# Linear attention with a mixture of adapters on one core: another spread of a batch's 576 tokens over the partitions, and other places for its loads

## The chip, the cores and the metric

The kernel runs on one core of a Trainium2 chip. The metric is the device time of one execution in microseconds (us), as the median of several executions. The engines are PE (TensorE), DVE (VectorE), ACT (ScalarE), POOL (GpSimd) and SP (SyncE, which here only issues transfers).

## What is computed

Two stages in a row, cut from the reference. The first is linear attention with position weights over 8 batches, 8 heads, 576 tokens and a head size of 64; the second is a gated mixture of 8 adapters of rank 16, of which the two with the highest logits count.

```python
def phi(x, c, s):                       # c, s: cos and sin of the position
    r = np.maximum(x, 0.0)
    return np.concatenate([r * c, r * s], axis=-1)
q_p, k_p = phi(q, cos_w, sin_w), phi(k, cos_w, sin_w)
kv = np.einsum('bhsf,bhsd->bhfd', k_p, v)
z = np.sum(k_p, axis=2)
num = np.einsum('bhsf,bhfd->bhsd', q_p, kv)
den = np.einsum('bhsf,bhf->bhs', q_p, z)[..., None] + 1e-06
attn = num / den                        # -> x, (4608, 512)
...
logits = x @ w_gate                     # 8 experts, the top two kept
w = softmax of the two kept logits
out = x + sum over the two: w * ((x @ A[e]) @ B[e])
```

The inputs q, k and v have 9.44 MB each in float32, and the output has 9.44 MB as well.

## The kernel before

**Tiling.** Two batches form a pair, and there are four pairs. A pair has 9 slots; a slot is one token on each of the 128 partitions. `NS` = 9 slots times four pairs make 36 slots, and the main loop goes through them with the index n. The 576 tokens of a batch are spread over 64 partitions: `LONG` = 5 consecutive tokens on each partition of one half, and `SHORT` = 4 on each partition of the other half. The batch with the even number has the lower half in slots 0 to 4 and the upper half in slots 0 to 3; the odd one has the upper half in slots 4 to 8 and the lower half in slots 5 to 8. So slot 4 is shared by both batches, and a slot's work needs one batch, or in slot 4 two.

**Loads.** `load` (L73) issues two transfers for each of k, q and v of a batch (L75): one to 64 partitions with 8 heads of 5 x 64 elements, and one to the other 64 with 8 heads of 4 x 64. One packet is one run of a head in one partition, so k and q move in packets of 1280 and 1024 bytes. k and q go over SP's queue (q1 in the profile) as float32. v goes over POOL's queue (q0) and is cast to bf16 on the way, so its packets read as many bytes as those of k and write half (640 and 512 bytes, which is what the profile counts for q0). The adapter weights A, w_gate and B go over ACT's queue (q10); A moves in packets of 64 bytes.

**Buffers and issue.** The pools for k and q have two buffers, each for a pair, and there are two v buffers, so the loads of pair m wait until pair m-2 is used up. The table `load_at` says at the end of which iteration n the loads of a batch are issued: batches 2 to 7 after n = 0, 2, 6, 10, 15 and 19. SP works its list in order: a load that stands behind a store isn't issued before the store, and a store waits for ACT's copy `osb` (L315). Besides, the transfers of SP and ACT carry eight completion semaphores in turn (DMAHW0 to DMAHW7), and the issuing engine waits before each transfer until the one eight places before it has landed.

**One iteration.** POOL scales q of slot n+3 by the cos and sin tables (`scale_q`, L190); ACT does the same with relu for k (`scale_k`, L149 and L154) of slot n+8, so ACT runs eight slots ahead and is the first to need a new batch; PE adds slot n+6 to the sums (`kv`, L172), transposes q (L198), multiplies (`numden`, L218); DVE moves the transposes out of PSUM (L203, L239) and divides (`normalise`, L225 and L227). Three slots form a group for the gate (`logits`, `gate_a`, `gate_sig`, `gate_b`). Some six slots after `normalise` a slot gets its adapters (`delta`, L306), ACT copies it out (`evac_o`, L315) and SP stores it (`store`, L327) in two transfers of 64 partitions, in packets of 2048 bytes.

**The head.** Before the loop stand the first loads, the position tables (`sin_tab`, `cos_tab`, L104 and L105, on ACT), the weights, and slots 0 to 4 of k, of which slot 4 needs both batches. DVE copies the weights to bf16 there (`AW` L347, `Ball` L348).

Of the kernel before, what the change touches and what calls it, by code (L numbers as in the profile page):

```python
# [19 lines left out]
LONG, SHORT = 5, 4  # L20
# [4 lines left out]
def kernel(ctx, tc, q, k, v, w_gate, A, Bw, out):  # L25
# [11 lines left out]
    LS = LONG * HALF  # L37
    assert S == LS + SHORT * HALF

# [13 lines left out]

    pos = persist.tile([128, NS], mybir.dt.int32, name="pos")
    lo, hi = slice(0, HALF), slice(HALF, 128)
    nc.gpsimd.iota(pos[lo, 0:5], pattern=[[1, 5]], base=0, channel_multiplier=LONG)
    nc.gpsimd.iota(pos[hi, 0:4], pattern=[[1, 4]], base=LS, channel_multiplier=SHORT)
    nc.gpsimd.iota(pos[lo, 5:9], pattern=[[1, 4]], base=LS, channel_multiplier=SHORT)
    nc.gpsimd.iota(pos[hi, 4:9], pattern=[[1, 5]], base=0, channel_multiplier=LONG)
# [4 lines left out]
    def halves(b):  # L64

        if b % 2 == 0:
            return ((lo, 0, LONG, 0), (hi, 0, SHORT, LS))
        return ((hi, 4, LONG, 0), (lo, 5, SHORT, LS))

    def part(dram, b, n, t0):  # L70
        return dram[b, :, t0:t0 + n * HALF, :].rearrange("h (p s) d -> p h s d", s=n)

    def load(eng, dram, t, b):  # L73
        for pr, s0, n, t0 in halves(b):
            eng.dma_start(out=t[pr, :, s0:s0 + n, :], in_=part(dram, b, n, t0))  # L75
# [4 lines left out]
    def load_k(b):  # L80
        m = b // 2
        if b % 2 == 0:
            k_t[m] = p_k.tile([128, H, NS, D], FP32, name="ks")
        load(nc.sync, k, k_t[m], b)

    def load_q(b):
        m = b // 2
        if b % 2 == 0:
            q_t[m] = p_q.tile([128, H, NS, D], FP32, name="qs")
        load(nc.sync, q, q_t[m], b)  # L90

    def load_v(b):
        load(nc.gpsimd, v, v_view(b // 2), b)

    load_k(0)
    load_v(0)
    load_q(0)
# [25 lines left out]

    AWf = persist.tile([128, DCH, ZW], FP32, name="AWf")
    for ci in range(DCH):
        nc.scalar.dma_start(out=AWf[:, ci, 0:ER],
                            in_=A[:, ci * 128:(ci + 1) * 128, :].transpose([1, 0, 2]))
    nc.scalar.dma_start(out=AWf[:, :, ER:ZW], in_=w_gate.rearrange("(c p) e -> p c e", p=128))
    Bf = persist.tile([128, DM], FP32, name="Bf")
    nc.scalar.dma_start(out=Bf, in_=Bw.rearrange("e r d -> (e r) d"))  # L130
    AW = persist.tile([128, DCH, ZW], BF16, name="AW")
    Ball = persist.tile([128, DM], BF16, name="Ball")

    load_k(1)
    load_v(1)
    load_q(1)


# [180 lines left out]
    def store(n):  # L319
        m, s = divmod(n, NS)  # L320
        t = osb_t.pop(n)
        for b in (2 * m, 2 * m + 1):
            for pr, s0, cnt, t0 in halves(b):
                if s0 <= s < s0 + cnt:
                    rows = out[b * S + t0:b * S + t0 + cnt * HALF, :].rearrange(
                        "(p s) d -> p s d", s=cnt)[:, s - s0, :]
                    nc.sync.dma_start(out=rows, in_=t[pr, :])  # L327

# [7 lines left out]
    load_at = {0: 2, 2: 3, 6: 4, 10: 5, 15: 6, 19: 7}  # L336

    with tc.manual_schedule():
        scale_q(0)
        scale_q(1)  # L340
        for j in range(5):
            scale_k(j, both=True)
            kv(j)
        transp_q(0)
        evac_q(0)
        kv_out(0)
        nc.vector.tensor_copy(AW, AWf)  # L347
        nc.vector.tensor_copy(Ball, Bf)  # L348
        scale_q(2)
        transp_q(1)  # L350
        numden(0)

        todo = []
        for n in range(NT + 8):
            live = n < NT
            ready = [g for g, t in enumerate(groups) if t[-1] + 1 == n]
            gated = [g for g, t in enumerate(groups) if t[-1] + 2 == n]
            moved = [g for g, t in enumerate(groups) if t[-1] + 3 == n]
            for g in ready:
                logits(g)  # L360
            for g in gated:
                gate_sig(g)
            if n + 3 < NT:
                scale_q(n + 3)
            if live:
                normalise(n)
            for j in scale_at.get(n, ()):
                if j < NT:
                    scale_k(j)
            for d in todo[:1] if live else todo:  # L370
                delta(d)
                evac_o(d)
                store(d)
            del todo[:1 if live else None]
            if live:
                transp_x(n)
            if n + 1 < NT:
                evac_q(n + 1)
                numden(n + 1)
            if live:  # L380
                evac_x(n)
            if n + 2 < NT:
                transp_q(n + 2)
            for g in moved:
                evac_z(g)
                todo += groups[g]
            for g in ready:
                gate_a(g)
            for g in gated:
                gate_b(g)  # L390
                transp_z(g)
            for j in kv_at.get(n, ()):
                if j < NT:
                    kv(j)
                    if j % NS in (4, 8):
                        kv_out(2 * (j // NS) + (j % NS == 8))
# [36 lines left out]
```

## Time and profile before

| | us |
|---|---|
| median of 3 executions | 165.33 (163.04 to 167.11) |
| the profiled execution, its own time | 166.19 |
| its span, first to last instruction | 164.4 |
| PE, DVE, ACT, POOL busy | 104.3, 89.5, 73.0, 61.4 |

The profiled execution is 1.8 us longer than its span and 0.9 us longer than the median. The share of the DMA engines in the profile is the sum of the times of all packets over 16 engines; packets of several queues, and packets that follow each other in one queue, can overlap, so it goes beyond 100%. The granted TensorE clock was 0.886 in the mean.

### The profile page before, as it was taken

The numbers are of one execution on the slowest core, as the hardware profiler recorded it, in microseconds if no ns is written. First come the engines' busy times: TensorE is split into PE (matmuls) and PEld (weight loads), VectorE is DVE, ScalarE is ACT, GpSimd is POOL, SyncE is SP. The second block draws the span as 40 slices with busy tenths as digits, with TensorE's granted clock in tenths as the row PEclk, the third lists the DMA queues.
The fourth block names the chain that finished last, engine by engine and source line by source line (L and its number), as shares of the span: only waits on it lengthen the run. The fifth ranks groups of instructions, "written<-read, shape, count | busy, mean of one in ns | idle before, by whom it ended". The sixth has DMA issues, their size and how long they took to land. (4 is left out here: it accounts for less than half of the span.)

```text
span 164.4 us, 3588 instructions
## 1 busy us (share of the span) xinstructions
PE 104.3 (63%) x1379; PEld 83.4 (51%) x1396; DVE 89.5 (54%) x273; ACT 73.0 (44%) x130; POOL 61.4 (37%) x98
## 2 busy tenths in 40 slices
PE   0000835994496698598398760198989897956450
PEld 0000834793496476486387640086868685733100
DVE  1001226852388376589368490058897889985200
ACT  3005439038803863683475500557578323213330
POOL 7100458770367057347433660033645363000000
PEclk9999999999559789999959996569999999996755
DMA  5999999999999999999999999999998664452654
GB/s 106 202 257 249 254 242 225 215 249 240 203 237 214 207 255 224 215 262 267 224 224 250 177 233 226 222 314 209 226 241 255 157 157 109 97 128 68 159 121 106
DMA packets 35953, 33.81 MB, mean 206 GB/s; under 512 B 6624, under 2 KB 31200, under 8 KB 35936
## 3 DMA queue, kind: packets, MB, share of 16 engines
q1 hardware_dynamic: 22656, 28.32, 75.3%
q0 software_dynamic: 8448, 4.72, 21.1%
q10 hardware_dynamic: 4832, 0.54, 2.9%
q8 instruction: 11, 0.18, 0.5%
q14 instruction: 6, 0.05, 0.1%
HBM read 28.85 MB, written 9.44 MB: 233 GB/s over the span
## 5 line engine op out<-in xcount | busy, mean ns | idle before, releaser
L190 POOL TENSOR_SCALAR qp<-qs,cos_tab 128x512 bf16<-128x512 f32 x36 | 25.0, 695 | 76.2 <-PE qpTp L198 52.3
L149 ACT ACTIVATE kp<-ks,cos_tab 128x512 bf16<-128x512 f32 x36 | 25.6, 718 | 38.9 <-DMA ks<-in_k_dram 33.4
L172 PE MATMUL kvz<-v,kp 128*128 128x128 bf16 (+1 forms) x320 | 28.4, 246 | 21.6 <-ACT kp L149 16.7
L172 PEld LDWEIGHTS <-kp 128*128 128x128 bf16 (+1 forms) x320 | 23.1, 111 | 23.4 <-ACT kp L149 19.7
L239 DVE COPY xT<-xz 128x512 bf16<-128x512 bf16 x36 | 15.2, 422 | 35.4 <-PE xz L234 34.9
L315 ACT COPY osb<-dx 128x512 f32<-128x512 f32 x36 | 20.7, 576 | 21.1 <-DMA out_dram<-osb 6.7
L306 PE MATMUL dx<-xt,ident 128*128 128x512 bf16 x35 | 14.9, 425 | 19.0 <-ACT osb L315 19.0
L198 PE MATMUL qpTp<-ident,qp 128*128 128x128 bf16 x288 | 25.4, 239 | 0.8 <-DVE qpT L203 0.8
L203 DVE TENSOR_SCALAR qpT<-qpTp 128x1024 bf16<-128x1024 bf16 x36 | 24.5, 682 | 2.2 <-PE qpTp L198 2.2
L227 DVE TENSOR_TENSOR xt<-nd,rden 128x512 bf16<-128x512 f32 x36 | 24.9, 692 | 1.2
L190 POOL TENSOR_SCALAR qp<-qs,sin_tab 128x512 bf16<-128x512 f32 x36 | 25.4, 706 | 0.0
L154 ACT ACTIVATE kp<-ks,sin_tab 128x512 bf16<-128x512 f32 x31 | 22.0, 708 | 0.0
L218 PE MATMUL nd<-kvsb,qpT 128*128 128x65 bf16 (+1 forms) x320 | 18.5, 204 | 4.1 <-ACT kvsb L184 2.3
L198 PEld LDWEIGHTS <-qp 128*128 128x128 bf16 x288 | 19.5, 108 | 1.3 <-issue 1.1
L234 PE MATMUL xz<-ident,xt 128*128 128x128 bf16 x144 | 16.1, 242 | 6.1 <-DVE xt L227 5.0
L234 PEld LDWEIGHTS <-xt 128*128 128x128 bf16 x144 | 11.6, 109 | 15.3 <-DVE xt L227 9.6
L218 PEld LDWEIGHTS <-qpT 128*128 128x128 bf16 (+1 forms) x320 | 14.1, 105 | 6.2 <-DVE qpT L203 3.0
L307 PEld LDWEIGHTS <-zgT 128*128 128x128 bf16 x36 | 3.7, 103 | 21.5 <-issue 21.4
L151 DVE TENSOR_SCALAR kp<-ks,sin_tab 128x512 bf16<-128x512 f32 x5 | 2.6, 565 | 18.6 <-ACT sin_tab L104 14.0
L214 PE MATMUL nd<-eps_hi,ones 128*128 128x4 bf16 x72 | 12.6, 177 | 0.0
L251 PE MATMUL za<-AW,xT 128*128 128x136 bf16 x144 | 11.0, 226 | 0.5 <-DVE xT L239 0.5
L75 POOL DMA_DIRECT2D v<-in_v_dram x16 | 11.2, 704 | 0.0
(41 smaller groups left out, 83.2 us busy)
## 6 DMA issues: line engine op xcount, KB each, us to landing
out_dram<-osb SPq DMA_DIRECT2D x72, 128.0 KB, 3.4
ks<-in_k_dram SPq DMA_DIRECT2D x8, 640.0 KB, 8.3
qs<-in_q_dram SPq DMA_DIRECT2D x8, 640.0 KB, 12.2
ks<-in_k_dram SPq DMA_DIRECT2D x8, 512.0 KB, 9.7
qs<-in_q_dram SPq DMA_DIRECT2D x8, 512.0 KB, 14.3
v<-in_v_dram POOLq DMA_DIRECT2D x8, 320.0 KB, 12.0
v<-in_v_dram POOLq DMA_DIRECT2D x8, 256.0 KB, 14.1
AWf<-in_moe_A_dram ACTq DMA_DIRECT2D x4, 64.0 KB, 9.6
```

Of the source, the lines that this page charges most:

```text
L149: nc.scalar.activation(kp[:, :, 0, :], src, AF.Relu, bias=0.0, scale=cos_tab[:, s:s + 1])
L154: nc.scalar.activation(kp[:, :, 1, :], src, AF.Relu, bias=0.0, scale=sin_tab[:, s:s + 1])
L172: nc.tensor.matmul(out=kvz_t[b][:, gg, jj], lhsT=kp_t[j][pr, h], rhs=v_rhs(m, h, s, pr), start=(first and jj == 0), stop=(last and jj == 3))
L190: nc.gpsimd.tensor_scalar(out=qp[:, :, i, :], in0=q_t[m][:, :, s, :], scalar1=tab[:, s:s + 1], scalar2=1.0, op0=ALU.mult, op1=ALU.mult)
L198: nc.tensor.transpose(out=t[:, h, :], in_=qp[:, h], identity=ident)
L203: nc.vector.tensor_scalar(out=t, in0=src, scalar1=0.0, scalar2=None, op0=ALU.max)
L218: nc.tensor.matmul(out=nd[pr, gg, j * W:(j + 1) * W], lhsT=qpT[:, gg * 4 + j, pr], rhs=kv_t[b][:, gg * 4 + j, :], start=False, stop=(j == ...
L227: nc.vector.tensor_tensor(out=xt, in0=nd[:, :, :, 0:D], in1=rden.rearrange("p (g j) -> p g j", g=2).to_broadcast([128, 2, 4, D]), op=ALU.mult)
L234: nc.tensor.transpose(out=xz[:, c * 128:(c + 1) * 128], in_=xt_t[n][:, c * 128:(c + 1) * 128], identity=ident)
L239: nc.vector.tensor_copy(t, xz[:, 0:512].rearrange("p (c s) -> p c s", c=DCH))
L306: nc.tensor.matmul(out=dx, lhsT=ident, rhs=xt_t.pop(n), start=True, stop=False)
L315: nc.scalar.copy(t, src)
```

## The change

A batch's first 512 tokens (`TAIL` = 512) go four to a partition over all 128 partitions: slots 0 to 3 for the even batch of a pair, slots 5 to 8 for the odd one. Its last 64 tokens go one to a partition into slot 4, the even batch's to the lower half, the odd one's to the upper half. A load becomes `load_main` (128 partitions, 8 heads of 4 x 64 elements, packets of 1024 bytes) and `load_tail` (64 partitions, 8 heads of 64 elements, packets of 256 bytes; for v 512 and 128 bytes as written). A slot's store is one transfer of 128 partitions, but for slot 4. The weights go over SP's queue behind the first k, v and q. `load_at` has the loads of batches 3 to 7 one or three iterations sooner. The copies of the weights to bf16 stand at the end of iteration 1. All instructions, those of the head too, now stand in the order in which they are written.

```diff
-LONG, SHORT = 5, 4
+FOUR = 4
...
-    def load(eng, dram, t, b):
-        for pr, s0, n, t0 in halves(b):
-            eng.dma_start(out=t[pr, :, s0:s0 + n, :], in_=part(dram, b, n, t0))
+    def load_main(eng, dram, t, b):
+        s0 = 0 if b % 2 == 0 else 5
+        eng.dma_start(out=t[:, :, s0:s0 + FOUR, :],
+                      in_=dram[b, :, 0:TAIL, :].rearrange("h (p s) d -> p h s d", s=FOUR))
+
+    def load_tail(eng, dram, t, b):
+        eng.dma_start(out=t[lo if b % 2 == 0 else hi, :, 4, :],
+                      in_=dram[b, :, TAIL:S, :].rearrange("h p d -> p h d"))
...
-    load_k(0)
-    load_v(0)
-    load_q(0)
+    load_main(nc.sync, k, k_t[0], 0)
+    load_main(nc.gpsimd, v, v_view(0), 0)
+    load_tail(nc.sync, k, k_t[0], 0)
+    load_tail(nc.sync, k, k_t[0], 1)
+    load_tail(nc.gpsimd, v, v_view(0), 0)
+    load_main(nc.sync, q, q_t[0], 0)
...
+    load_main(nc.sync, k, k_t[0], 1)
+    load_tail(nc.gpsimd, v, v_view(0), 1)
+    load_main(nc.gpsimd, v, v_view(0), 1)
+    load_tail(nc.sync, q, q_t[0], 0)
+    load_tail(nc.sync, q, q_t[0], 1)
     AWf = persist.tile([128, DCH, ZW], FP32, name="AWf")
     for ci in range(DCH):
-        nc.scalar.dma_start(out=AWf[:, ci, 0:ER],
+        nc.sync.dma_start(out=AWf[:, ci, 0:ER],
...
+    load_main(nc.sync, q, q_t[0], 1)
...
+        if s == 4:
+            for b, pr in ((2 * m, lo), (2 * m + 1, hi)):
+                nc.sync.dma_start(out=out[b * S + TAIL:(b + 1) * S, :], in_=t[pr, :])
+        else:
+            b, i = (2 * m, s) if s < 4 else (2 * m + 1, s - 5)
+            rows = out[b * S:b * S + TAIL, :].rearrange("(p s) d -> p s d", s=FOUR)[:, i, :]
+            nc.sync.dma_start(out=rows, in_=t)
...
-    load_at = {0: 2, 2: 3, 6: 4, 10: 5, 15: 6, 19: 7}
+    load_at = {0: 2, 1: 3, 3: 4, 7: 5, 12: 6, 16: 7}
...
+        if n == 1:
+            nc.vector.tensor_copy(AW, AWf)
+            nc.vector.tensor_copy(Ball, Bf)
         if n in load_at:
...
+            first, then = (load_main, load_tail)[::1 if b % 2 == 0 else -1]
+            for eng, dram, t in ((nc.sync, k, k_t[m]), (nc.gpsimd, v, v_view(m)),
+                                 (nc.sync, q, q_t[m])):
+                first(eng, dram, t, b)
+                then(eng, dram, t, b)
```

The first place where the order differs is the head of SP's list (`ks` and `qs` are the tiles of k and q, the numbers behind them partitions x heads x elements, and DMAHW0 to DMAHW7 the completion semaphores, `_49` being a part of their names). Before, eight loads of half a batch:

```order
L75 DMA ks<-in_k_dram 64x8x320
L75 DMA ks<-in_k_dram 64x8x256
L75 DMA qs<-in_q_dram 64x8x320 [waits DMAHW0_49]
L75 DMA qs<-in_q_dram 64x8x256 [waits DMAHW1_49]
L75 DMA ks<-in_k_dram 64x8x320 [waits DMAHW2_49]
L75 DMA ks<-in_k_dram 64x8x256 [waits DMAHW3_49]
L75 DMA qs<-in_q_dram 64x8x320 [waits DMAHW4_49]
L75 DMA qs<-in_q_dram 64x8x256 [waits DMAHW5_49]
```

After:

```order
L69 DMA ks<-in_k_dram 128x8x256
L73 DMA ks<-in_k_dram 64x8x64 x2
L69 DMA qs<-in_q_dram 128x8x256
L69 DMA ks<-in_k_dram 128x8x256
L73 DMA qs<-in_q_dram 64x8x64 x2
L123 DMA AWf<-in_moe_A_dram 128x8x16
L123 DMA AWf<-in_moe_A_dram 128x8x16 [waits DMAHW0_49]
L123 DMA AWf<-in_moe_A_dram 128x8x16 [waits DMAHW1_49]
L123 DMA AWf<-in_moe_A_dram 128x8x16 [waits DMAHW2_49]
L125 DMA AWf<-in_moe_w_gate_dram 128x4x8 [waits DMAHW3_49]
L127 DMA Bf<-in_moe_B_dram 128x512 [waits DMAHW4_49]
L69 DMA qs<-in_q_dram 128x8x256 [waits DMAHW5_49]
```

The weights have moved from ACT's list to SP's, behind the first k, the first q and the second k; the transfer of B (`Bf`) is the thirteenth of the list, and so waits for the fifth, the second batch's k, to land. Before, the second k waited for the weights' transfers, since ACT's and SP's share the eight semaphores.

The second place is the end of SP's list, around the loads of the last batch. Before (`osb` is a finished slot):

```order
L327 DMA out_dram<-osb 64x512 x8
L75 DMA ks<-in_k_dram 64x8x320
L75 DMA ks<-in_k_dram 64x8x256
L75 DMA qs<-in_q_dram 64x8x320
L75 DMA qs<-in_q_dram 64x8x256
L327 DMA out_dram<-osb 64x512 x44
```

After:

```order
L322 DMA out_dram<-osb 128x512 x4
L73 DMA ks<-in_k_dram 64x8x64
L69 DMA ks<-in_k_dram 128x8x256
L73 DMA qs<-in_q_dram 64x8x64
L69 DMA qs<-in_q_dram 128x8x256
L322 DMA out_dram<-osb 128x512 x2
L318 DMA out_dram<-osb 64x512 x2
```

Before, 44 stores of half a slot, 22 slots, stand behind the last load, and so 14 slots ahead of it; after, 25 slots stand behind it and 11 ahead.

The third place is DVE's list around the first divisions. Before, the copies of the weights stand ahead of the first of them:

```order
L203 TENSOR_SCALAR qpT<-qpTp 128x1024
L347 CAST AW<-AWf 128x544
L348 CAST Ball<-Bf 128x512
L225 RECIPROCAL rden<-nd 128x8
L227 TENSOR_TENSOR xt<-nd,rden 128x512
```

After, they stand behind the second slot:

```order
L219 RECIPROCAL rden<-nd 128x8
L221 TENSOR_TENSOR xt<-nd,rden 128x512
L197 TENSOR_SCALAR qpT<-qpTp 128x1024
L233 COPY xT<-xz 128x512
L389 CAST AW<-AWf 128x544
L390 CAST Ball<-Bf 128x512
L219 RECIPROCAL rden<-nd 128x8
```

They moved past two slots of DVE's work, and what waits behind them now is the third slot's division.

## Rows read from the trace of the kernel before

**Rows 1.** The page: DMA in 40 slices, packets, queues.

```profile
DMA  5999999999999999999999999999998664452654
GB/s 106 202 257 249 254 242 225 215 249 240 203 237 214 207 255 224 215 262 267 224 224 250 177 233 226 222 314 209 226 241 255 157 157 109 97 128 68 159 121 106
...
q1 hardware_dynamic: 22656, 28.32, 75.3%
q0 software_dynamic: 8448, 4.72, 21.1%
q10 hardware_dynamic: 4832, 0.54, 2.9%
```

**Rows 2.** Stretches: busy us (x instructions) of PE, PEld, DVE, ACT, POOL; PEclk, DMA share, GB/s.

```profile
100.00:107.00 7.00, 0.59 (x1) 0.25 (x2) 0.00 (x0) 2.51 (x5) 0.00 (x0) 0.50 1.12 222
130.00:146.00 16.00, 13.22 (x206) 10.26 (x210) 14.63 (x44) 4.61 (x10) 4.25 (x7) 1.00 0.56 128
```

**Rows 3.** All waits of the engines: us in total, times, longest.

```profile
ACT kp L149 <- DMA ks<-in_k_dram: 33.4, 10, 9.5
```

**Rows 4.** Timeline of ACT: start, length, instruction, idle before it and its releaser.

```profile
104.49 0.72 ACT L149 ACTIVATE kp<-ks,cos_tab 128x512 bf16<-128x512 f32 x1 [9.47 <-DMA ks<-in_k_dram]
...
118.59 0.72 ACT L149 ACTIVATE kp<-ks,cos_tab 128x512 bf16<-128x512 f32 x1 [0.62 <-DMA ks<-in_k_dram]
```

**Rows 5.** Timeline of DVE: the divisions of slots 0, 22 and 35.

```profile
27.36 0.21 DVE L225 RECIPROCAL rden<-nd 128x8 f32<-128x8 f32 x1 [0.84 <-PE nd L218]
...
112.52 0.20 DVE L225 RECIPROCAL rden<-nd 128x8 f32<-128x8 f32 x1
...
146.70 0.20 DVE L225 RECIPROCAL rden<-nd 128x8 f32<-128x8 f32 x1
```

**Rows 6.** DMA queues from 100 to 107 us: packets, MB, share of 16 engines.

```profile
q1 hardware_dynamic: 1404, 1.55, 111.9%
```

**Rows 7.** DMA queues from 8 to 16 us.

```profile
q0 software_dynamic: 1171, 0.66, 57.1%
q1 hardware_dynamic: 1171, 1.30, 56.3%
q10 hardware_dynamic: 1170, 0.07, 10.4%
```

**Rows 8.** DMA queues from 88 to 91 us.

```profile
q1 hardware_dynamic: 415, 0.63, 69.9%
q0 software_dynamic: 431, 0.22, 53.0%
```

**Rows 9.** DMA queues from the start to 118.6 us.

```profile
q1 hardware_dynamic: 18357, 21.72, 81.0%
q0 software_dynamic: 8448, 4.72, 29.2%
q10 hardware_dynamic: 4832, 0.54, 4.0%
```

**Rows 10.** DMA queues from 91 to 96 us.

```profile
q0 software_dynamic: 504, 0.31, 62.2%
q1 hardware_dynamic: 324, 0.52, 31.9%
```

**Rows 11.** Timeline of SP: its last loads of k.

```profile
93.24 1.94 SPq L75 DMA_DIRECT2D ks<-in_k_dram  x2
...
110.08 1.97 SPq L75 DMA_DIRECT2D ks<-in_k_dram  x2
```

**Rows 12.** Timeline of the head, 0 to 45 us.

```profile
10.76 3.36 ACTq L130 DMA_DIRECT2D Bf<-in_moe_B_dram  x1
...
15.88 2.56 ACT L149 ACTIVATE kp<-ks,cos_tab 128x512 bf16<-128x512 f32 x4
...
29.63 0.21 DVE L225 RECIPROCAL rden<-nd 128x8 f32<-128x8 f32 x1 [0.21 <-PE nd L218]
```

**Rows 13.** The stores' line: ns of one issue, minimum, median, maximum.

```profile
L327 SPq DMA_DIRECT2D out_dram<-osb x72: 466/542/1697, 55.0 to 161.0; - x72
```

**Rows 14.** POOL's loads of v: busy us, mean ns.

```profile
L75 POOL DMA_DIRECT2D v<-in_v_dram x16 | 11.2, 704 | 0.0
```

More of the change, by code (lines that the diff above doesn't have):

```diff
@@ L36 @@
     NT = PAIRS * NS
[L37 to L38 removed]
+    TAIL = FOUR * 128
+    assert S == TAIL + HALF
     persist = ctx.enter_context(tc.tile_pool(name="persist", bufs=1))
@@ L59 @@
-    nc.gpsimd.iota(pos[hi, 4:9], pattern=[[1, 5]], base=0, channel_multiplier=LONG)
+    nc.gpsimd.iota(pos[:, 0:4], pattern=[[1, 4]], base=0, channel_multiplier=FOUR)
+    nc.gpsimd.iota(pos[:, 5:9], pattern=[[1, 4]], base=0, channel_multiplier=FOUR)
+    nc.gpsimd.iota(pos[lo, 4:5], pattern=[[0, 1]], base=TAIL, channel_multiplier=1)
+    nc.gpsimd.iota(pos[hi, 4:5], pattern=[[0, 1]], base=TAIL, channel_multiplier=1)
     k_t, q_t, v_t = {}, {}, {}
     v_bufs = [persist.tile([128, H * NS * D + D], BF16, name=f"v{i}") for i in range(2)]
[L64 to L68, printed above, removed]
@@ L335 @@
         kv_at[n] = [n + 6]
-    load_at = {0: 2, 2: 3, 6: 4, 10: 5, 15: 6, 19: 7}
[L338 to L396, printed above, removed]
-            if n in load_at:
-                b = load_at[n]
-                load_k(b)
-                load_v(b)
-                load_q(b)
-        assert not todo
@@ new lines @@
+    load_at = {0: 2, 1: 3, 3: 4, 7: 5, 12: 6, 16: 7}
+    scale_q(0)
+    scale_q(1)
+    for j in range(5):
+        scale_k(j, both=True)
+        kv(j)
+    transp_q(0)
+    evac_q(0)
+    kv_out(0)
+    scale_q(2)
+    transp_q(1)
+    numden(0)
+    todo = []
+    for n in range(NT + 8):
+        live = n < NT
+        ready = [g for g, t in enumerate(groups) if t[-1] + 1 == n]
+        gated = [g for g, t in enumerate(groups) if t[-1] + 2 == n]
+        moved = [g for g, t in enumerate(groups) if t[-1] + 3 == n]
+        for g in ready:
+            logits(g)
+        for g in gated:
+            gate_sig(g)
+        if n + 3 < NT:
+            scale_q(n + 3)
+        if live:
+            normalise(n)
+        for j in scale_at.get(n, ()):
+            if j < NT:
+                scale_k(j)
+        for d in todo[:1] if live else todo:
+            delta(d)
+            evac_o(d)
+            store(d)
+        del todo[:1 if live else None]
+        if live:
+            transp_x(n)
+        if n + 1 < NT:
+            evac_q(n + 1)
+            numden(n + 1)
+        if live:
+            evac_x(n)
+        if n + 2 < NT:
+            transp_q(n + 2)
+        for g in moved:
+            evac_z(g)
+            todo += groups[g]
+        for g in ready:
+            gate_a(g)
+        for g in gated:
+            gate_b(g)
+            transp_z(g)
+        for j in kv_at.get(n, ()):
+            if j < NT:
+                kv(j)
+                if j % NS in (4, 8):
+                    kv_out(2 * (j // NS) + (j % NS == 8))
+        if n == 1:
+            nc.vector.tensor_copy(AW, AWf)
+            nc.vector.tensor_copy(Ball, Bf)
+        if n in load_at:
+            b = load_at[n]
+            m = b // 2
+            if b % 2 == 0:
+                new_pair(m)
+            first, then = (load_main, load_tail)[::1 if b % 2 == 0 else -1]
[3 more added lines that the diff above has]
+                then(eng, dram, t, b)
@@ L406 @@
+    assert not todo
 _INS = ['q', 'k', 'v', 'moe_w_gate', 'moe_A', 'moe_B']
```

37 lines of the change are left out of this document (8 added, 29 removed).

## The prediction
> **What bounds the kernel now.** I read the page's slices first. The DMA engines are busy from the second slice on and stay so for some 30 of the 40, while no compute engine comes near that; only in the last ten does the DMA row fall [rows 1]. Next I asked for stretches. Between 100 and 107 us PE did one matmul and DVE nothing, with the DMA share at 1.12; between 130 and 146 us, when no loads are left, DVE is busy for 14.63 of 16 us [rows 2]. So the kernel first waits for loads and then works at its own pace. The waits say for which loads: ACT, the engine that runs ahead, stood still for 33.4 us for k [rows 3], at one place for 9.47 us [rows 4]. The last such wait ends at 118.59 us, when the last batch's k has landed. From there on nothing waits for a load for long: the divisions of slots 22 and 35 are 34.18 us apart, 2.63 us a slot over 13 slots [rows 5], and the span ends 164.4 - 118.6 = 45.8 us after that k. So the time is the moment of the last k plus 45.8 us, and the sum below is about that moment.
>
> What sets it? Between 100 and 107 us only q1 moves anything, k and q alone: 1404 packets, 1.55 MB, 222 GB/s, and 1.119 x 16 x 7 us / 1404 = 89 ns a packet [rows 6]. Between 8 and 16 us the same kind of packet shares the engines with v, and takes 0.563 x 16 x 8 / 1171 = 61.5 ns, for 1.30 MB / 1171 = 1110 bytes [rows 7]. There v reads twice what it writes, so memory gives 1.30 + 1.32 + 0.07 MB in 8 us, 336 GB/s; between 88 and 91 us, stores beside v, it is 0.63 + 0.44 MB in 3 us, 357 GB/s [rows 8]. So 222 GB/s is the limit of neither the memory nor the engines. It is what 64-partition transfers get when they run alone, one half of the partitions after the other.
>
> [...]
>
> **The change part by part.**
>
> *128 partitions.* Up to 118.6 us q0 moved all its 4.72 MB [rows 9]; at 0.66 MB in 8 us [rows 7] that is 57 us of mixed traffic, in which q1 and q10 moved 57/8 x 1.37 = 9.8 MB. Of their 22.26 MB [rows 9] some 12.5 MB are left that ran alone: 56 us at 222 GB/s. 57 + 56 and some 2 us of start (the first slice is half busy [rows 1]) are 115 of the 118.6. Loads and stores alone at 128 partitions are not in the trace. The bounds are 222 GB/s (nothing gained) and 357 GB/s (35 us, 21 gained); the mixed packet's 1110 bytes in 61.5 ns on 16 engines are 288 GB/s (43 us, 13 gained). I take the mixed stretch's 336 GB/s, because both its queues together show what the engines carry when the halves don't stand against each other: 12.5 / 0.336 = 37 us, **-19 us**.
>
> *Tails.* New are 16 transfers of k and q with 64 x 8 = 512 packets of 256 bytes each, 512 packets for each of the 16 engines, and 8 of v, 256 per engine. The bytes were there before; what counts is the time above that of their bytes. For k and q that is 256 bytes at 336/16 = 21 bytes per ns, 12.2 ns. The nearest row is A's 64-byte packet: 0.104 x 16 x 8 us / 1170 = 11.4 ns [rows 7]; with 192 more bytes at the mixed packet's 18 bytes per ns a tail packet is 22 ns. (22 - 12.2) x 512 = 5.0 us. v's packets average 0.571 x 16 x 8 / 1171 = 62.4 ns for 576 written bytes [rows 7]; by bytes 128 are 13.9 ns, and with the same factor of 1.8 as for k they take 25 ns: 11 x 256 = 2.8 us, and in mixed traffic, whose share is 1.24, 2.3 us. Together **+7 us**. The bounds are 0 (bytes alone) and the price of a full packet, 61.5 and 62.4 ns: 49.3 x 512 + 48.5 x 256 / 1.24 = 35 us.
>
> *Loads sooner.* SP's list has 11 slots' stores ahead of the last k where 14 were: 3 x 0.262 MB / 336 GB/s = **-2.3 us** (between 0 and -3.5, at 222). Before, ACT's 9.47 us wait began with k not yet issued: SP got to it at 93.24 us [rows 11], behind stores that wait for ACT. The engines ran on with stores and v, but from 91 to 96 us at a share of 0.94 instead of 1.12 or 1.24 [rows 10]; filling that is **-1 us** (0 to -9.5, if the whole wait were a hole). Issued three iterations sooner, the next batch is queued while ACT still waits for the one before. What the earlier places wait for is there by then: pair 0's q is read by POOL up to three slots ahead, and its last load in SP's list holds back only the first stores, six slots later. POOL issues one main and one tail for v instead of two halves; at 0.70 us per issue [rows 14], and if a main of twice the packets took twice as long, 8 x 0.7 us more lie in POOL's idle time (it is busy 61 us).
>
> *Head.* ACT's transfers are gone; its tables waited behind B's, issued from 10.76 us on, and the first k was scaled at 15.88 us [rows 12]. Now that waits for k alone, and slot 4's k is loaded at once. I expect the first division about 6 us sooner than 27.36 us. None of it counts in the sum: the queues are full anyway, and ACT stands still later for the next k instead. If loads ceased to bind, it would be worth its 6 us. The weights' 0.54 MB are loaded either way.
>
> *The new wait.* The weights' copies on DVE now wait for B, whose issue waits for the second k to land. Ahead of that stand three mains, two tails and most of two batches of v, 5.6 MB, at 336 GB/s 17 us; with start, tails and A's packets B is there at some 25 us. The second slot should end at 24 to 26 us (6 us before the 29.63 plus its 2 us [rows 12]). So DVE waits 0 to 2 us, with the third slot's division behind it, then PE's transposes. Slot 4 needs the second batch anyway, so I count 0; at most +2.
>
> *The end.* The last slot's store is one transfer: an issue of 0.54 us less [rows 13], **-0.5 us**. The 25 slots behind the last load make fewer issues on SP, which has room.
>
> Sum: -19 + 7 - 2.3 - 1 - 0.5 = -15.8 us. The last k lands at about 103 us, the span is 148.6 us, the execution 148.6 + 1.8 = 150.4 us against the profiled 166.19; the median is 0.9 us below that one, so **150 us** to the nearest.
>
> **The rivals.** What a measurement of this kernel can tell from no change is 2%: faster is below 162.0, slower above 168.6 us.
>
> *A, dear small packets (slower).* Each tail packet costs as much time as a full one. Then +35 takes the place of +7: 150 + 28 = 178 us. It decides from the point where the tails eat the other 22.8 us, at 65% of the way, some 44 ns a tail packet. For it: such packets are not in the trace, and there is one to every two full ones. Against it: 64-byte packets took 11.4 ns between 8 and 16 us. [...]
>
> *B, the 222 GB/s are a queue's own (no gain).* One queue alone never gets more, whatever the partitions. Then -19 goes and the rest stays: 165.3 + 7 - 3.8 = 168.5 us, at the edge of slower. For it: every stretch of 222 has one queue alone. Against: the same queue's packets get shorter, 61.5 against 89 ns, as soon as the other queue takes half of the engines' time.
>
> *C, the loads stop binding (faster).* Then the first division at 21.4 us, 35 slots at 2.63 and the 17.7 us from the last division to the end give 131 us, with 0.9 us (1.8 - 0.9) 132 us. Against it: a slot loads and stores 1.05 MB, in 2.63 us 399 GB/s, more than the 357 of any row.
>
> **How the numbers follow.** Forecast 0.74, A 0.08, B 0.10, C 0.08. The forecast's own costs reach from 357 GB/s with tails at their bytes' price (150 - 2 - 7 = 141) to 288 GB/s with tails halfway to A's point (150 + 6 + 5 = 161). The range for 8 in 10 is 138 to 163 us: the forecast and the nearer parts of B and C. Faster gets the forecast without its upper edge, and C: 0.71 + 0.08 = 0.79, and 0.02 for a B whose tails cost little, 0.81; same gets 0.03 of the forecast and 0.07 of B, 0.10; slower gets A and the last of B, 0.09.
>
> **What would show it.** Right: stretches of q1 alone at 300 GB/s or more; k's main packets near 50 ns and tails near 22; the last wait of ACT for k ending near 103 us, and 45 to 46 us from there to the end; ACT still waiting for k over 10 us in all. Wrong: such stretches still at 222 (B); packets under 512 bytes at over 40 ns (A); no wait for k after the head (C). A wait of DVE for B beyond 2 us would show that I mispriced the head.

## The result, and the profile after

The changed kernel takes **151.93 us** (median of 4 executions, 151.37 to 152.99). The kernel before took 165.56 us on the same chip (4 executions, 163.04 to 167.11). The ratio is 0.9261, with a 95% interval from 0.9121 to 0.9401; here and below an execution that is over 1.5% slower than the fastest of its kernel is left out of a ratio, but not of a median. I forecast 150.0 us, in a range from 138 to 163. The profiled execution took 151.37 us, its span 149.3 us, at a granted clock of 0.885 (before 0.886).

The page of the changed kernel, the lines that answer to [rows 1]; a slice is now 3.73 us long:

```profile
DMA  3999999999999999999999999999731333232542
GB/s 98 277 222 274 260 197 144 164 318 348 286 251 261 304 311 220 313 307 265 254 331 286 247 276 338 283 286 382 271 142 70 108 107 127 88 140 75 159 170 92
...
q1 hardware_dynamic: 35168, 28.86, 67.1%
q0 software_dynamic: 12544, 4.72, 26.6%
```

The DMA engines are full up to the 28th slice, 104.5 us, and then the loads are through; before, the last k landed at 118.6 us [rows 4]. In the GB/s row the long stretches near 220 are gone. One hole has come: two slices at 144 and 164, from 22 to 30 us. A part of it is only in the count, since v moves there and counts half of the bytes that it reads.

The DMA queues, for four stretches in this order: from the start to 104.1 us, from 20 to 31 us, from 32 to 36 us, and from 31.4 to 42.2 us (packets, MB, share of 16 engines):

```profile
q1 hardware_dynamic: 31890, 22.98, 80.5%
q0 software_dynamic: 12544, 4.72, 38.2%
...
q0 software_dynamic: 3256, 1.24, 97.4%
q1 hardware_dynamic: 5461, 0.56, 45.7%
...
q1 hardware_dynamic: 1414, 1.43, 109.6%
...
q1 hardware_dynamic: 4316, 3.53, 111.8%
```

The line of 1414 packets answers to [rows 6]: again q1 alone, now 1.43 MB in 4 us, 358 GB/s where it was 222, and 1.096 x 16 x 4 / 1414 = 49.6 ns a packet where it was 89. These are nearly all main packets; the whole stretch without v, the last line, has tails as well, and 3.53 MB in 10.8 us are 327 GB/s. From 20 to 31 us q1 moved 0.56 MB in 5461 packets, 14.7 ns each: these are mostly A's packets of 64 bytes, and hardly any k or q. With v's 1.24 MB, for which 2.48 MB are read, the memory gave 3.04 MB in these 11 us, 276 GB/s.

The waits of ACT for loads of k ([rows 3]) and for a free output buffer, and below its timeline at the longest of them ([rows 4]):

```profile
ACT kp L143 <- DMA ks<-in_k_dram: 20.3, 3, 12.0
ACT osb L309 <- DMA out_dram<-osb: 10.1, 3, 8.0
```

Before, the second of these waits was shorter each time:

```profile
ACT osb L315 <- DMA out_dram<-osb: 6.7, 4, 2.7
```

After, at the longest of them:

```profile
39.05 0.72 ACT L143 ACTIVATE kp<-ks,cos_tab 128x512 bf16<-128x512 f32 x1 [12.03 <-DMA ks<-in_k_dram]
51.17 0.72 ACT L143 ACTIVATE kp<-ks,cos_tab 128x512 bf16<-128x512 f32 x1 [5.30 <-DMA ks<-in_k_dram]
80.11 0.59 ACT L309 COPY osb<-dx 128x512 f32<-128x512 f32 x1 [8.00 <-DMA out_dram<-osb]
```

ACT waits for k three times instead of ten, the last time until 51.17 us. Then comes a wait that the kernel before did not have at this length: the copy into an output buffer stands still for 8.00 us until a store has landed.

DVE's timeline: the divisions (RECIPROCAL) of slots 0, 2, 4, 8, 15, 16 and 35, and the copy of the weights ahead of slot 2's ([rows 5] and [rows 12]):

```profile
19.25 0.21 DVE L219 RECIPROCAL rden<-nd 128x8 f32<-128x8 f32 x1 [1.00 <-PE nd L212]
...
32.22 0.44 DVE L389 CAST AW<-AWf 128x544 bf16<-128x544 f32 x1 [8.63 <-DMA AWf<-in_moe_w_gate_dram]
...
32.97 0.20 DVE L219 RECIPROCAL rden<-nd 128x8 f32<-128x8 f32 x1
...
42.82 0.21 DVE L219 RECIPROCAL rden<-nd 128x8 f32<-128x8 f32 x1 [1.02 <-PE nd L212]
...
54.90 0.20 DVE L219 RECIPROCAL rden<-nd 128x8 f32<-128x8 f32 x1
...
73.60 0.20 DVE L219 RECIPROCAL rden<-nd 128x8 f32<-128x8 f32 x1
83.29 0.20 DVE L219 RECIPROCAL rden<-nd 128x8 f32<-128x8 f32 x1
...
134.26 0.20 DVE L219 RECIPROCAL rden<-nd 128x8 f32<-128x8 f32 x1
```

The first division is 8.1 us sooner than before, but slot 8's is only at 54.90: eight slots take 35.65 us. From slot 8 to slot 15 a slot takes 18.70 / 7 = 2.67 us, from 16 to 35 50.97 / 19 = 2.68 us; that is the engines' own pace, close to the 2.63 us of [rows 5]. Between slots 15 and 16 lie 9.69 us, the wait for a store. So the time now is: k of batch 3 at 51.17, slot 8 3.73 us later, 27 slots at the own pace, one stall of some 7 us, and the end.

Behind the last division come 15.0 us, where it was 17.7. The rows of these ends, first after, then before (busy us of the engines, then the granted clock, the DMA share and GB/s):

```profile
134.26:142.00 7.74, 4.27 (x32) 2.27 (x33) 4.11 (x20) 2.63 (x7) 0.00 (x0) 1.00 0.38 119
...
146.70:157.70 11.00, 6.43 (x33) 3.14 (x35) 4.11 (x20) 3.25 (x7) 0.00 (x0) 0.69 0.48 110
```

DVE does the same work in both, 4.11 us in 20 instructions, in 7.74 us at a clock of 1.00 after and in 11.00 us at 0.69 before. So up to 2.7 of the 15.1 us by which the span is shorter lie behind the last division, at another granted clock; how much of them belongs to the change no run tells.

SP's timeline, at the weights and at the first stores ([rows 11] before):

```profile
14.12 10.11 SPq L123 DMA_DIRECT2D AWf<-in_moe_A_dram  x4
24.27 2.49 SPq L125 DMA_DIRECT2D AWf<-in_moe_w_gate_dram  x1
26.80 0.59 SPq L127 DMA_DIRECT2D Bf<-in_moe_B_dram  x1
27.44 0.43 SPq L69 DMA_DIRECT2D qs<-in_q_dram  x1
27.91 0.96 SPq L69 DMA_DIRECT2D ks<-in_k_dram  x1
...
62.99 2.19 SPq L73 DMA_DIRECT2D qs<-in_q_dram  x1
65.22 1.65 SPq L69 DMA_DIRECT2D qs<-in_q_dram  x1
66.96 4.77 SPq L322 DMA_DIRECT2D out_dram<-osb  x2
71.82 1.31 SPq L318 DMA_DIRECT2D out_dram<-osb  x2
```

The six transfers of the weights hold SP from 14.12 to 27.39 us; the next large loads, q of batch 1 and k of batch 2, are issued only then. And the stores that ACT waits for at 72 us were issued from 66.96 us on, right behind loads of k and q that were still under way. The first of them is the one whose landing ends the wait at 80.11 us, some 13 us after its issue, where the median of the 32 is 3.5 us (from issue to landing):

```profile
DMA to landing us min/median/max: 2.0/3.5/13.1
```

### The profile page after: what moved, and what is told of

The parts are those of the page before. It is cut to its first block, busy times and chain, and to the rows that moved or that the text cites. A ratio compares the mean times of both kernels' runs of the same rounds, so it can differ in the third digit from the quotient of the medians.

```text
span 149.3 us, 3558 instructions
## 1 busy us (share of the span) xinstructions
PE 102.0 (68%) x1396; PEld 81.3 (54%) x1396; DVE 89.5 (60%) x273; ACT 71.6 (48%) x129; POOL 62.7 (42%) x98
## 5 line engine op out<-in xcount | busy, mean ns | idle before, releaser
L143 ACT ACTIVATE kp<-ks,cos_tab 128x512 bf16<-128x512 f32 x36 | 25.5, 716 | 28.6 <-DMA ks<-in_k_dram 20.3
L166 PEld LDWEIGHTS <-kp 128*128 128x128 bf16 (+1 forms) x320 | 23.6, 113 | 12.9 <-ACT kp L143 7.7
L192 PE MATMUL qpTp<-ident,qp 128*128 128x128 bf16 x288 | 24.1, 232 | 1.7 <-POOL qp L184 0.9
L184 POOL TENSOR_SCALAR qp<-qs,sin_tab 128x512 bf16<-128x512 f32 x36 | 24.9, 692 | 0.0
L228 PE MATMUL xz<-ident,xt 128*128 128x128 bf16 x144 | 15.2, 233 | 12.1 <-DVE xt L221 11.9
L228 PEld LDWEIGHTS <-xt 128*128 128x128 bf16 x144 | 10.8, 104 | 22.3 <-DVE xt L221 17.1
L300 PE MATMUL dx<-xt,ident 128*128 128x512 bf16 x36 | 14.3, 397 | 10.5 <-ACT osb L309 10.5
L192 PEld LDWEIGHTS <-qp 128*128 128x128 bf16 x288 | 18.5, 104 | 2.2 <-POOL qp L184 2.1
L212 PEld LDWEIGHTS <-qpT 128*128 128x128 bf16 (+1 forms) x320 | 13.4, 103 | 6.1 <-DVE qpT L197 3.0
L301 PE MATMUL dx<-Ball,zgT 128*128 128x512 bf16 x36 | 14.4, 400 | 0.0
L301 PEld LDWEIGHTS <-zgT 128*128 128x128 bf16 x36 | 3.6, 99 | 12.1 <-issue 12.1
L245 PEld LDWEIGHTS <-xT 128*128 128x128 bf16 x144 | 9.6, 102 | 0.7 <-DVE xT L233 0.7
## 6 DMA issues: line engine op xcount, KB each, us to landing
qs<-in_q_dram SPq DMA_DIRECT2D x8, 1024.0 KB, 12.5
```

The source lines that it names most:

```text
L143: nc.scalar.activation(kp[:, :, 0, :], src, AF.Relu, bias=0.0, scale=cos_tab[:, s:s + 1])
L166: nc.tensor.matmul(out=kvz_t[b][:, gg, jj], lhsT=kp_t[j][pr, h], rhs=v_rhs(m, h, s, pr), start=(first and jj == 0), stop=(last and jj == 3))
L184: nc.gpsimd.tensor_scalar(out=qp[:, :, i, :], in0=q_t[m][:, :, s, :], scalar1=tab[:, s:s + 1], scalar2=1.0, op0=ALU.mult, op1=ALU.mult)
L192: nc.tensor.transpose(out=t[:, h, :], in_=qp[:, h], identity=ident)
L212: nc.tensor.matmul(out=nd[pr, gg, j * W:(j + 1) * W], lhsT=qpT[:, gg * 4 + j, pr], rhs=kv_t[b][:, gg * 4 + j, :], start=False, stop=(j == ...
L228: nc.tensor.transpose(out=xz[:, c * 128:(c + 1) * 128], in_=xt_t[n][:, c * 128:(c + 1) * 128], identity=ident)
```

## The experiments

All runs change the changed kernel. Times are medians; a ratio is to the kernel before on the same chip, with its 95% interval. "Slot 8" and "slot 35" are the starts of these divisions in the profiled execution. The runs were on several chips, on which the kernel before took 164.16 to 165.56 us.

| run | us | ratio | slot 8 | slot 35 |
|---|---|---|---|---|
| changed kernel | 151.93 | 0.9261 (0.9121 to 0.9401) | 54.90 | 134.26 |
| halves of 64 partitions | 171.29 | none given | 62.56 | 152.78 |
| halves by heads | 154.10 | 0.9381 (0.9302 to 0.9460) | 56.63 | 136.06 |
| weights on ACT's queue | 154.16 | 0.9375 (0.9300 to 0.9450) | 56.23 | 135.67 |
| 14 output buffers | 148.25 | 0.9016 (0.8932 to 0.9100) | 54.71 | 129.40 |
| loads where they were | 151.88 | 0.9291 (0.9226 to 0.9356) | 53.63 | 132.98 |
| 14 buffers, weights on POOL's queue | 149.15 | 0.9112 (0.9029 to 0.9195) | 57.33 | 131.30 |
| 14 buffers, half of the loads | 144.25 | 0.8835 (0.8774 to 0.8896) | 54.60 | 127.16 |
| tails of k and q twice | 169.49 | 1.0288 (1.0184 to 1.0393) | 62.60 | 150.74 |
| 14 buffers, q one batch later | 144.89 | none given | 51.90 | 126.79 |
| the same, once more | 145.39 | 0.8836 (0.8779 to 0.8893) | 53.88 | 128.12 |
| the same, weights on POOL's queue | 145.71 | 0.8885 (0.8787 to 0.8984) | 53.27 | 128.78 |
| 6 buffers, q one batch later | 151.50 | 0.9204 (0.9140 to 0.9268) | not read | not read |

**Is it the 128 partitions?** One run issues each main load as two transfers of 64 partitions, a control as two of 128 partitions with four heads each.

```diff
+        for pr in (lo, hi):
+            eng.dma_start(out=t[pr, :, s0:s0 + FOUR, :], in_=src[pr])
```

> Each main load of 128 partitions is issued as two transfers of 64 partitions each, one after the other; bytes, packets of 1024 bytes and everything else as in the changed kernel. Theory (the gain is that one transfer spans all 128 partitions): stretches in which k and q move alone fall back from about 350 to about 220 GB/s, their packets go from about 50 to over 75 ns, and the time goes to 162 to 170 us. Rival (the gain is packet size, sooner loads or order): 150 to 155 us and 340 GB/s or more in such stretches.

```diff
+        for hh in (slice(0, 4), slice(4, 8)):
+            eng.dma_start(out=t[:, hh, s0:s0 + FOUR, :], in_=src[:, hh])
```

> The control for the kernel in two halves: each main load is issued as two transfers of 128 partitions, heads 0 to 3 and heads 4 to 7. As many transfers, semaphore waits and bytes per transfer as there. Theory: within 3 us of the changed kernel's 151.9, stretches of k and q alone at 330 GB/s or more. Rival (more transfers on eight semaphores are what costs): as slow as the kernel in two halves, 160 us or more.

The halves of partitions took 171.29 us (168.17 to 173.43), slower than the kernel before on that chip (164.25). The halves by heads took 154.10 us, within the 3 us expected. From the trace of the first, at a granted clock of 0.832, I read only what the DMA engines moved. Its GB/s row on the page, slices of 4.24 us, and q1 in a stretch without v of each run, from 53.2 to 61.8 us with halves of partitions and from 49.8 to 55.8 us with halves by heads:

```profile
GB/s 98 234 203 258 271 132 193 228 209 212 217 215 227 206 216 228 221 230 269 240 212 290 254 229 212 321 257 199 295 286 107 109 80 126 121 128 65 111 137 124
...
q1 hardware_dynamic: 2228, 1.82, 113.2%
...
q1 hardware_dynamic: 2153, 1.80, 111.9%
```

From the 8th slice to the 18th it never leaves 206 to 230 GB/s, where the changed kernel has up to 348. Without v, k and q moved at 1.82 / 8.6 = 212 GB/s, in the control at 1.80 / 6.0 = 300 (330 was expected; about a quarter of the packets of both are tails). In the packet records of the two traces a main packet took 75.8 ns in the mean, and 56.0 in the control. The number of transfers isn't the cause, since the control has as many. So the spread over 128 partitions is worth 168.17 - 154.10 = 14 us by the fastest execution with halves, 17 us by the medians. In the packet records of the kernel before, the halves of its loads move one after the other, as I had it: from 103.5 to 105.5 us q1 has 352 packets of 1280 bytes and none of 1024, from 106.5 to 108.0 us 337 of 1024 bytes and none of 1280.

**The weights' wait.** B and A go over ACT's queue right behind the tables, w_gate stays on SP's.

```diff
-        nc.sync.dma_start(out=AWf[:, ci, 0:ER],
+        nc.scalar.dma_start(out=AWf[:, ci, 0:ER],
...
-    nc.sync.dma_start(out=Bf, in_=Bw.rearrange("e r d -> (e r) d"))
+    nc.scalar.dma_start(out=Bf, in_=Bw.rearrange("e r d -> (e r) d"))
```

> The weights A and B go over ACT's queue right behind its tables, w_gate over SP's behind the first q tails. Theory (in the changed kernel A's small packets in SP's queue hold up the loads behind them between 20 and 31 us, and DVE waits 8.6 us for the weights): the wait of DVE before the copy of the weights falls below 2 us, the third division comes near 25 us instead of 33, and the time falls by 4 to 8 us, to 144 to 148. Rival (the loads are the limit anyway and the wait only moves): 150 to 153 us with more waiting for k or q later.

It took 154.16 us: the theory fell, and the time is a little above the rival's range as well. The timeline of its head:

```profile
6.91 8.62 ACTq L120 DMA_DIRECT2D AWf<-in_moe_A_dram  x2
...
27.51 0.45 DVE L389 CAST AW<-AWf 128x544 bf16<-128x544 f32 x1
```

DVE doesn't wait any more, but ACT spends 8.62 us on the issue of two transfers and scales its first k at 15.58 us instead of 6.89; slot 8 comes at 56.23 us instead of 54.90. The wait of DVE lay beside another one: ACT waits for k until 51.88 us here, and slot 8's division follows this by 4.35 us.

**The store's wait.** The pool of output buffers gets 14 instead of 6.

```diff
-    p_o = ctx.enter_context(tc.tile_pool(name="p_o", bufs=6))
+    p_o = ctx.enter_context(tc.tile_pool(name="p_o", bufs=14))
```

> Fourteen buffers for the finished slots instead of six. Theory (in the changed kernel ACT waits 8.0 us at 72 to 80 us for a buffer whose store lies in SP's queue behind loads, and the work runs at its own pace from then on): that wait is gone and the time falls by 4 to 7 us, to 145 to 148. Rival (the loads are the limit there): ACT or POOL waits as long for k or q instead, 150 to 153 us.

It took 148.25 us, as expected. The wait for stores is gone, and slot 16 comes at 76.58 us instead of 83.29. ACT's timeline past 60 us, waits for transfers:

```profile
88.90 0.72 ACT L143 ACTIVATE kp<-ks,cos_tab 128x512 bf16<-128x512 f32 x1 [3.44 <-DMA ks<-in_k_dram]
...
100.53 0.72 ACT L143 ACTIVATE kp<-ks,cos_tab 128x512 bf16<-128x512 f32 x1 [0.86 <-DMA ks<-in_k_dram]
```

Of the 6.71 us won at slot 16 4.86 us are left at slot 35, since ACT now runs into k, 4.3 us in all. The loads stand just behind the stores' wait. Of these 4.86 us the span keeps 2.6, because 17.3 us come behind the last division instead of 15.0, at a granted clock of 0.56 in their first 7.74 us, where it was 1.00:

```profile
129.40:137.14 7.74, 5.74 (x29) 2.66 (x29) 3.13 (x16) 2.13 (x5) 0.00 (x0) 0.56 0.20 73
```

**The sooner loads.** The table of the loads as before the change.

```diff
-    load_at = {0: 2, 1: 3, 3: 4, 7: 5, 12: 6, 16: 7}
+    load_at = {0: 2, 2: 3, 6: 4, 10: 5, 15: 6, 19: 7}
```

> The changed kernel with the loads of batches 3 to 6 issued where they were before the change (after slots 2, 6, 10 and 15 instead of 1, 3, 7 and 12, and the last after slot 19 instead of 16). My prediction's sum gave 3.3 us of gain to the sooner loads (2.3 us for stores, 1 us for holes), in a kernel that a load bounds to the end: by it this one takes 154 to 157 us. Rival: past 51 us the loads bind little, and the sooner loads stand in SP's list ahead of stores, which the copies into the six output buffers then wait for (8.00 us); issued later, the loads let the stores pass, that wait shrinks, and the time is 149 to 152 us, no longer than the changed kernel's.

It took 151.88 us, a ratio of 0.9291 beside 0.9261; the rival held. ACT's waits and its last wait for k:

```profile
ACT kp L143 <- DMA ks<-in_k_dram: 36.3, 11, 10.0
...
ACT osb L309 <- DMA out_dram<-osb: 0.2, 1, 0.2
```

```profile
105.19 0.72 ACT L143 ACTIVATE kp<-ks,cos_tab 128x512 bf16<-128x512 f32 x1 [1.88 <-DMA ks<-in_k_dram]
```

With the loads later the stores aren't waited for, and k is instead, up to 105.19 us. This also shows what the stores stood behind. The two waits change places at the same price, as far as the intervals tell. Slot 8's division (53.63 us) follows ACT's last wait for k before it, which ends at 49.89 us, by 3.74 us, as in the changed kernel (3.73).

**Weights on POOL's queue, with 14 buffers.** The same six transfers behind v of batch 1, the copies one slot later.

```diff
-        nc.sync.dma_start(out=AWf[:, ci, 0:ER],
+        nc.gpsimd.dma_start(out=AWf[:, ci, 0:ER],
...
-        if n == 1:
+        if n == 2:
             nc.vector.tensor_copy(AW, AWf)
```

> The changed kernel with 14 output buffers, the expert weights and the gate on POOL's queue behind the v loads of batch 1 instead of on SP's ahead of q of batch 1, and the two copies of the weights one slot later (after slot 2). With 14 output buffers alone the kernel took 148.25 us and had three waits at the head: 7.2 us of DVE for the weights, 11.5 us of ACT for k of batch 2, 10.3 us of POOL for q. Theory: all three come from the weights' 4096 packets of 64 bytes, which hold up what SP's queue has behind them; on a queue of their own they delay no k or q, k of batch 2 lands at 32 to 35 us instead of 39, and the time is 142 to 146 us. Rival: the same packets only take turns with others, the head is bound by the bytes of the first three batches, the wait moves to v or to the weights themselves, and the time stays at 147 to 150 us.

It took 149.15 us, in the rival's range, though no row shows packets taking turns. k of batch 2 is there at 37.33 us and DVE waits for no weight, yet slot 8 comes at 57.33, again 4.35 us behind a wait of ACT for k that ends at 52.98. Two ways to take the weights' wait away gained nothing; each brought a cost of its own, so the price of the wait alone isn't shown.

**Do loads bound the second half?** The loads of batches 4 to 7 are left out, and the second half computes from the first half's data.

```diff
+            if b >= 4:
+                k_t[m], q_t[m] = k_t[m % 2], q_t[m % 2]
+                continue
```

> The changed kernel with 14 output buffers and without the loads of batches 4 to 7 (k, v and q): the second half of the work reads the tiles of the first half again, so the output is another. It asks whether the load stream still bounds the second half. Theory: past slot 17 the engines' own pace of about 3 us a slot bounds it, and loads cost no more than the 4.3 us that ACT still waited for k after 60 us with 14 buffers: 143 to 148 us, against 148.25. Rival, as my prediction's sum has it (the time is the landing of the last k and a fixed rest): without the loads that land between 60 and 104 us the end comes far sooner, at 125 to 138 us.

It took 144.25 us, as the theory has it: 4.0 us less than with 14 buffers alone, though half of the loads are gone. The page:

```profile
DMA  4999999999999932224141223332114323132631
GB/s 119 254 199 274 261 241 138 165 235 360 295 301 305 280 118 78 76 95 132 74 151 75 78 107 95 97 130 95 76 74 152 74 99 129 74 152 98 196 146 75
```

From the 16th slice on only stores are left, and the pace is (127.16 - 54.60) / 27 = 2.69 us a slot all the same. Up to slot 8 nothing is changed: 54.60 us.

**The price of a tail.** Each tail of k and of q is loaded a second time into a tile that nothing reads.

```diff
+        if eng is nc.sync:
+            again = spare["k" if dram is k else "q"][b // 2]
+            eng.dma_start(out=again[lo if b % 2 == 0 else hi, :, :],
+                          in_=dram[b, :, TAIL:S, :].rearrange("h p d -> p h d"))
```

> The changed kernel with each tail of k and of q loaded a second time, into tiles that nothing reads: 8192 more packets of 256 bytes. At the 22 ns that such a packet took they add 180 us of packet time, 11.3 us on 16 engines. If the load stream bounded the whole time, as in my prediction's sum, the end would come about 11 us later: 161 to 165 us. Theory now: the loads bound the time only up to about 51 us, by which some half of the tails have been loaded, so 154 to 159 us. Rival, dear small packets (44 ns and more when there are more of them): 22 us of engine time or more, 165 us and over.

It took 169.49 us (167.48 to 172.57): my theory fell, and the time lies where the rival with dear packets had it. Its DMA queues up to 120.6 us, when its loads were through:

```profile
q1 hardware_dynamic: 40133, 24.71, 85.7%
q0 software_dynamic: 12544, 4.72, 32.7%
```

q1's packets took 0.857 x 16 x 120.6 = 1654 us, against 0.805 x 16 x 104.1 = 1341 us in the changed kernel: 313 us for 8192 packets more, 38 ns each. The packet records of the two traces divide this: a tail packet took 26.7 ns in the mean instead of 22.3, which is 31 ns for each that was added, and a main packet 58.7 instead of 55.5. That is less than the rival's 44 ns, but far above 22. The number of transfers alone doesn't explain it: the control by heads issues 16 transfers more on SP's queue too, and took 2.2 us more than the changed kernel. The loads end 16.5 us later (120.6 against 104.1), and the profiled execution 17.0 us (168.36 against 151.37). Slot 8 comes 7.7 us later (62.60); the stall at slot 16 grows by 4.1 us (slots 15 and 16 at 82.20 and 95.95); from there to slot 35 a slot takes 54.79 / 19 = 2.88 us instead of 2.68, 3.8 us in all. So with six buffers the loads can't be slowed without the end feeling it nearly in full, though with 14 buffers taking half of them away gives only 4 us: stream and engines are nearly level.

**A version that uses this.** With 14 buffers, q of a batch is issued behind k and v of the next one, so that k of batch 2 doesn't stand behind q of batch 1, nor k of batch 3 behind q of batch 2.

```diff
-            for eng, dram, t in ((nc.sync, k, k_t[m]), (nc.gpsimd, v, v_view(m)),
-                                 (nc.sync, q, q_t[m])):
+            for eng, dram, t in ((nc.sync, k, k_t[m]), (nc.gpsimd, v, v_view(m))):
                 first(eng, dram, t, b)
                 then(eng, dram, t, b)
+            load_q(b - 1)
+            if b == 7:
+                load_q(b)
```

> The changed kernel with 14 output buffers and each q load from batch 1 on issued one batch later, behind k and v of the next batch (q of batch 1 behind k and v of batch 2, and so on; the last two at the end). Theory: the time is the landing of k of batch 3, which ACT waits for last (51.17 us in the changed kernel), plus the engines' own 2.7 us for each of the slots 8 to 35 and 15 us behind the last division; with q of batch 2 behind it, k of batch 3 lands some 4 us sooner, slot 8 begins at about 51 us instead of 55, and the time is 142 to 146 us, against 148.25 with 14 buffers alone. Rival: the bytes that a slot needs are the same in either order, POOL waits for q where ACT waited for k, and the time stays at 147 to 150 us.

> The kernel with 14 output buffers and q one batch later once more, for an interval: its first four runs lay between 143.31 and 146.71 us. Theory: 143 to 147 us, 0.87 to 0.90 of the time before. Rival: the gain over 14 buffers alone was chance, and the time is 147 to 149 us.

The first time it took 144.89 us (143.31 to 146.71), the second 145.39 us (144.85 to 147.98), ratio 0.8836 (0.8779 to 0.8893). The first run's waits of POOL and ACT for loads of q and k:

```profile
POOL qp L194 <- DMA qs<-in_q_dram: 34.2, 6, 14.2
ACT kp L153 <- DMA ks<-in_k_dram: 16.6, 3, 9.7
```

```profile
51.90 0.20 DVE L229 RECIPROCAL rden<-nd 128x8 f32<-128x8 f32 x1
...
126.79 0.20 DVE L229 RECIPROCAL rden<-nd 128x8 f32<-128x8 f32 x1
```

ACT's last wait for k now ends at 36.04 us. In this first run slot 8 comes 2.8 us sooner than with 14 buffers alone and slot 35 2.6 us sooner; in the second it is 0.8 and 1.3 us. The time is the theory's, the way to it only in part: with 14 buffers alone ACT's last wait for k ahead of slot 8 was already the one for batch 2, until 39.58 us, and part of ACT's wait has moved to POOL, for q, as the rival had it. The rest of the gain lies behind the last division, 14.9 and 15.4 us against 17.3, where no k or q is loaded and the run with 14 buffers had the low clock of 0.56. So the two edits together are faster than 14 buffers alone by their intervals (0.8779 to 0.8893 against 0.8932 to 0.9100), but how much of this the order of q gives stays open. The ratio is that of the run with half of the loads, 0.8835. It is the fastest version of this study that does all of the work, and faster than both kernels.

Two variants of it:

> The same as the run of q one batch later, with the weights on POOL's queue behind v of batch 1 and their copies after slot 2. Theory: the weights' 64-byte packets cost time on the 16 engines wherever they are queued and only the order at the head changes; so within 2 us of the run of q later alone, 141 to 147 us. Rival: with q out of the way of k, the wait for the weights is what is left at the head, and taking the weights off SP's queue gives 3 us or more on top.

> The changed kernel with its six output buffers and q loaded one batch later. In the changed kernel the copies into the output buffers waited 8.00 us for stores that stood in SP's list behind loads of q that wait for a free tile. Theory: with q later SP gets to the stores sooner, and the order of q alone gives most of what it and 14 buffers gave together: 144 to 148 us. Rival: the stores stand behind loads all the same, the wait of 8 us stays, and the time is 149 us or more.

With the weights on POOL's queue it took 145.71 us (ratio 0.8885, 0.8787 to 0.8984), in the theory's range. With six output buffers it took 151.5 us, ratio 0.9204 (0.9140 to 0.9268), where the rival had it: the order of q alone gives nothing that can be told from the changed kernel, so the buffers are needed for what the two give together. In the changed kernel's trace q's loads hardly wait for a free tile: SP waits for POOL's work on q once, 0.7 us. Whether the wait for stores is what eats the gain stays open: the trace of this run is of an execution of 174.2 us, at a granted clock of 0.584, and shows nothing of it.

## Why the prediction was right, and where not

The time, 150.0 against 151.93 us, was right, and its largest term was right for the reason given. One step of the argument was not, and the sum survived it because two limits lie close together.

- **128 partitions, -19 us.** Right. Main packets alone ran at 358 GB/s and the whole stretch with tails at 327, on both sides of the 336 that I took; with these the term is 12.5 / 0.222 - 12.5 / 0.358 = -21 us, or -18. The run with halves of partitions gives back 14 to 17 us against its control.
- **Tails, +7 us.** Undersized, as far as the doubled tails tell. The changed kernel's packet records show 22.3 ns for a tail packet of k or q, as I worked out. But a second set of tails lengthened q1's packet time by 38 ns for each, and the loads by 16.5 us, where 22 ns gave 11. Less 8192 x 12.2 ns / 16 = 6.2 us for the bytes that leaves 10 us where I had 5.0 for k and q. It is the price of a second set behind the first; no run takes the first set away, so its own price isn't shown, nor what made up for it. Rival A's 44 ns was not reached.
- **"The last k lands at about 103 us".** Right, as far as the rows tell: its load was issued at 92.14 us and the DMA engines are full up to 104.5. Nothing waits for it, so the landing itself isn't seen as a wait.
- **"So the time is the moment of the last k plus 45.8 us".** This is the step that failed. The last wait for k ended at 51.17 us, not near 103, and at 103 us nothing stood still for k. From 51.17 us on the engines went at their own 2.68 us a slot and were held up once, by stores. That the span still ends 149.3 - 103 = 46 us behind the last k is a coincidence of two nearly equal rates: the loads take (104.5 - 2) / 8 = 12.8 us a batch, the engines 4.5 x 2.68 = 12.1 us. The 2.7 us fewer behind the last division, where my sum had 0.5, are part of the coincidence. The run with half of the loads, 4.0 us faster only, shows that the loads had ceased to set the second half. Rival C was half true: I had set it against the bandwidth of one slot and didn't see that loads which run ahead for eight slots need to keep up only in the mean. Its sign, no wait for k after the head, came true past 51.17 us. Its 132 us were missed by the head, where slot 8 waits for four batches (54.90 us instead of 19.25 + 8 x 2.68 = 40.7), and by the stores' wait.
- **Loads sooner, -2.3 and -1 us.** Not there: the run with the later loads took 151.88 us against 151.93. What failed is the sentence that a load in SP's list "holds back only the first stores": behind those stores stand six output buffers, ACT's copy, and through it PE and DVE, 8.00 us. With 14 buffers the sooner loads take 148.25 us, 3.7 less; no run has 14 buffers and the later loads, so whether the sooner loads are then worth anything isn't shown.
- **The new wait, 0 to 2 us.** It was 8.63 us, and by my own sign I had mispriced the head: I had B at 25 us, but SP issued it at 26.80 and DVE got on at 32.2, because SP's list stood at A for 10.11 us. That it counts 0 fits all the same: slot 4's division (42.82) follows the wait of ACT for k of batch 2 (39.05) by 3.8 us, by 4.0 in the two runs without the wait, and these were no faster.
- **The head, counted 0.** Right. The first division came 8.1 us sooner (I expected 6), and ACT then stood 12.03 us for k of batch 2. The weights on ACT's queue, with the first division at 23.26 us instead of 19.25, cost slot 8 only 1.3 us. Of the last store's -0.5 us no run tells anything.
- **The other signs.** ACT still waited 20.3 us for k (over 10 expected), and k's and q's main packets took 49.6 ns without v (near 50 expected; 55.5 over the whole run).

## What to carry to other kernels

A sum of "the last load plus a fixed rest" holds only as long as the loads are the slower stream; work out both rates, per batch here 12.8 us of loads and 12.1 us of engines, because the gain of a faster load ends where they meet. With the loads issued one or three iterations sooner, on the queue that also carries the stores, ACT stood 10.1 us for stores here, and 0.2 us with the later loads: count the output buffers that must bridge this. When a wait is taken away, first look for the next one beside it; here nothing was gained where the weights' 8.63 us were taken away, and 3.7 us where the stores' 8.00 us were.

## What the runs showed of the hardware beyond that

- While A's small packets were in q1, that queue moved little: from 20 to 31 us it had 5461 packets in the record but moved 0.56 MB, while v's packets on q0 took 0.974 x 16 x 11 / 3256 = 52.6 ns each. How much of this is the small packets' doing isn't shown: SP issued its next large loads only from 27.44 us on, and no run separates the two.
- Issuing can stop an engine that computes: two of A's transfers held ACT for 8.62 us, where all four took POOL 3.54 us in the run with 14 buffers and the weights on POOL's queue.
- A set of tails loaded right behind another cost more packet time than the first set's own packets show, 38 against 22 ns for each (31 of them in the tails, the rest in the main packets). Why is open.
